# Sixteen rows of a weight matrix loaded early by GpSimd, to shift work between the DMA engines of a decode attention kernel

## The chip, the cores and the metric

The program runs on one core of one Trainium2 chip. The time is the device time of that core for one execution, in microseconds (us), as the median of several runs. The "span" of a profile runs from the first to the last instruction and is some 2 us shorter than the device time.

## The reference

One query token goes through grouped attention over a cache of 65,536 keys, and in parallel through a small dense layer. Cut to what matters:

```python
# x: (1, 1, 512); k_cache, v_cache: (1, 8, 65536, 128); wq: (512, 4096); wo: (4096, 512); all bf16
xn = layernorm(x)
q  = (xn @ wq) as 32 heads of 128          # 4 query heads share one K/V head
p  = softmax(q . k * 128**-0.5)
o  = p . v                                 # 32 x 128
out = x + o.reshape(4096) @ wo + dense_gelu(xn)
```

K and V are 268 MB, all weights together 12 MB. Nothing is used twice, so the kernel has to read 280.5 MB from HBM, the chip's main memory, once.

## The kernel before

SyncE (SP) issues all large loads in one order: K part, K part, V pair, and so on, and wo last. K has two slots and V two slots in one large buffer. The first slots of the same buffer take wo at the end, when K no longer needs them:

```python
    # WP = [(0, 4), (4, 2), (6, 1)]: wo arrives in parts of 16, 8 and 4 rows of 512 values for each partition
    wo_sb = kv[:, 0:GE * HPG * D].rearrange("p (r n) -> p r n", n=D)
    ...
    def dma_wo():
        for i, (g0, n) in enumerate(WP):
            r = n * HPG
            sch.dma(SP, lambda g0=g0, n=n, r=r: sp.dma_start(
                out=wo_sb[:, g0 * HPG:g0 * HPG + r, :],
                in_=A_wo[g0 * HPG * DH:(g0 + n) * HPG * DH, :].rearrange("(p r) n -> p r n", r=r)),
                wsem[i], writes=[f"wo{i}"] + (["slot0"] if i == 0 else []))
        # ... two small parts for the last K/V head follow
```

So the first part of wo is 128 rows of 16 KB each (the packet record of the kernel before has them as 128 packets of 16,384 bytes), one for each of the 128 partitions that the kernel uses in the on-chip buffer that loads are written to, SBUF. GpSimd (POOL) does nothing in the loop but a tiny memset (0.09 us), a "flag", when the second half of a V pair has landed. TensorE reads that half only after the flag:

```python
    def ready_v(res):
        sch.op(POOL, lambda: pool.memset(flag[:, :], 0.0), reads=[res], writes=["v_odd"])
```

The times of the flags are therefore a good clock: one for each of the 16 pairs of K and V.

Of the kernel before, what the change touches and what calls it, by code (L numbers as in the profile page):

```python
# [5 lines left out]
BF = mybir.dt.bfloat16  # L6
# [231 lines left out]
def bass_parallel_sum__gqa_block_cached__dense_activation_gelu__decode_kernel(  # L238
# [13 lines left out]
    D = A_x.shape[-1]  # L252
    DH = 128
    H = A_wq.shape[1] // DH
    G = A_k_cache.shape[1]
    HPG = H // G
# [25 lines left out]
    sch = _Sched(nc)  # L282
# [3 lines left out]
    POOL = sch.add_engine("pool", "pool")  # L286
    SP = sch.add_engine("sp", "sp")
# [7 lines left out]
    pool = nc.gpsimd  # L295
    sp = nc.sync

    def sb(name, shape, dt):
        return nc.alloc_sbuf_tensor(name, shape, dt)
# [25 lines left out]
    kv = sb("kv", [128, NSLOT * TPD * DH], BF)  # L325
# [8 lines left out]
    GE = G - 1  # L334
    WP = []
    g0 = 0
    while g0 < GE:
        n = next(m for m in (4, 2, 1) if g0 + m <= GE)
        WP.append((g0, n))
        g0 += n  # L340
    wo_sb = kv[:, 0:GE * HPG * D].rearrange("p (r n) -> p r n", n=D)
    wl_at = TPD * DH
    wl_sb = kv[:, wl_at:wl_at + HPG * D].rearrange("p (h n) -> p h n", h=HPG)
    kt_ring = sb("kt_ring", [128, NKT * BCOL], BF)
# [20 lines left out]
    oX_bf = sb("oX_bf", [128, GE * HPG], BF)  # L365
# [21 lines left out]
    sem_w2 = sch.dsem("dw2")  # L387
    wsem = [sch.dsem(f"wsem{i}") for i in range(len(WP))]
    lsem = [sch.dsem(f"lsem{i}") for i in range(2)]
    sem_vb = sch.dsem("dvb")  # L390
    sem_out = sch.dsem("dout")

    sch.op(POOL, lambda: pool.memset(sums_all[:, :], 1.0), writes=["sums_all"])
    for t, res in ((ident_bf, "ident_bf"), (ident_f, "ident_f")):
# [4 lines left out]
                out=t[:, :], in_=t[:, :], compare_op=ALU.not_equal, fill=1.0,  # L399
# [49 lines left out]
    def done_chunk(b):  # L449
        free.add(b)  # L450
        issue_chunks()
# [20 lines left out]

    WH = (HPG - 1, 1)

    def dma_wo():
        for i, (g0, n) in enumerate(WP):
            r = n * HPG
            sch.dma(SP, lambda g0=g0, n=n, r=r: sp.dma_start(
                out=wo_sb[:, g0 * HPG:g0 * HPG + r, :],
                in_=A_wo[g0 * HPG * DH:(g0 + n) * HPG * DH, :].rearrange("(p r) n -> p r n", r=r)),  # L480
                wsem[i], writes=[f"wo{i}"] + (["slot0"] if i == 0 else []))
        h0 = 0
        for i, n in enumerate(WH):
            sch.dma(SP, lambda h0=h0, n=n: sp.dma_start(
                out=wl_sb[:, h0:h0 + n, :],
                in_=A_wo[(H - HPG + h0) * DH:(H - HPG + h0 + n) * DH, :].rearrange("(h p) n -> p h n", p=128)),
                lsem[i], writes=[f"wl{i}"] + (["slot1"] if i == 0 else []))
            h0 += n
# [94 lines left out]
    def transposes(b, s):  # L583
        blk = b * BPC + s
        for t in range(TPB):
            fill = (blk * TPB + t) // 8
            tb, at = fill % NPT, t % 8
            sch.op(
                PE,
                lambda tb=tb, at=at, b=b, tt=s * TPB + t: pe.transpose(  # L590
                    pst[tb][:, at * 128:(at + 1) * 128], slot[b][:, tt, :], ident_bf[:, :]),
                reads=[f"slot{b}", "ident_bf"], writes=[f"pst{tb}"], publish=at == 7,
            )
            if at == 7:
                kb, q = blk % NKT, t // 8
                dst = kt_ring[:, kb * BCOL + q * 1024:kb * BCOL + (q + 1) * 1024]
                if fill % 8 in (0, 2, 3, 5, 6):
                    e, fn = DVE, lambda tb=tb, dst=dst: dve.tensor_copy(out=dst, in_=pst[tb][:, :])  # L598
                else:
                    e, fn = ACT, lambda tb=tb, dst=dst: act.activation(out=dst, in_=pst[tb][:, :],  # L600
                                                                      func=ACTF.Copy)
                sch.op(e, fn, reads=[f"pst{tb}"], writes=[f"kt{kb}_{q}"])
# [28 lines left out]
    def load_q(i):  # L631
        sch.op(DVE, lambda: dve.tensor_copy(out=q_cur[:, :], in_=qT_bf[:, at_pair(i, HPG, 0, HPG)]),
               reads=["qT"], writes=["q_cur"])


    def stats_1():
        sch.op(PE, lambda: pe.matmul(pA[0:HPG, PA_ST:PA_ST + 128], lhsT=pmax[:, 0:HPG], rhs=ident_f[:, :],  # L637
                                     start=True, stop=True), reads=["pmax", "ident_f"], writes=["pA"])
        sch.op(DVE, lambda: dve.tensor_reduce(out=gmax4[:, :], in_=pA[0:HPG, PA_ST:PA_ST + 128], axis=AX.X,  # L639
                                              op=ALU.max), reads=["pA"], writes=["gmax"])  # L640
        sch.op(DVE, lambda: dve.tensor_scalar(out=diag4[:, :], in0=ident_f[0:HPG, 0:HPG],  # L641
                                              scalar1=gmax4[0:HPG, 0:1], scalar2=None, op0=ALU.mult),
               reads=["gmax", "ident_f"], writes=["diag"])

    def stats_2(u):
        k = u % 2
        us = slice(k * HPG, (k + 1) * HPG)
        sch.op(PE, lambda: pe.matmul(pA[:, PA_SB:PA_SB + HPG], lhsT=ones_f[0:HPG, 0:128],  # L648
                                     rhs=diag4[0:HPG, 0:HPG], start=True, stop=True),
               reads=["diag", "ones_f"], writes=["pA"])  # L650
        sch.op(DVE, lambda us=us: dve.tensor_scalar(out=negm[:, us], in0=pA[:, PA_SB:PA_SB + HPG],  # L651
                                                    scalar1=-1.0, scalar2=None, op0=ALU.mult),
               reads=["pA"], writes=[f"negm{k}"])
        src = pss[k][:, 0:CW].rearrange("p (t j) -> p t j", j=HPG)
        for j in range(HPG):
            at = k * HPG + j
            sch.op(
                ACT,
                lambda k=k, at=at, j=j, src=src: act.activation(  # L659
                    out=P_v[k][:, :, j], in_=src[:, :, j], func=ACTF.Exp,  # L660
                    bias=negm[:, at:at + 1], scale=1.0, accum_out=sums[:, at:at + 1]),
                reads=[f"negm{k}", f"pss{k}"],
                writes=[f"P{k}_{j}", f"sums{at}"],
            )
        if k:
            i = u // 2
            sch.op(DVE, lambda: dve.tensor_copy(out=negm_all[:, at_pair(i, PW, 0, PW)], in_=negm[:, :]),
                   reads=["negm0", "negm1"], writes=["negm_all"])
# [3 lines left out]
    def keep_sums(i):  # L672
        sch.op(DVE, lambda: dve.tensor_copy(out=sums_all[:, at_pair(i, PW, 0, PW)], in_=sums[:, :]),  # L673
               reads=[f"sums{at}" for at in range(PW)], writes=["sums_all"])
# [21 lines left out]
    def total():  # L696
        sch.op(PE, lambda: pe.matmul(pA[:, PA_SUM:PA_SUM + NC], lhsT=ones_f[:, :], rhs=sums_all[:, :],  # L697
                                     start=True, stop=True), reads=["ones_f", "sums_all"], writes=["pA_sum"])
# [40 lines left out]
    def body(i):  # L739
        last = i == NU // 2 - 1  # L740
        for b in range(2):
            u = 2 * i + b
            transposes(b, 0)
            if b:
                stats_1()
            transposes(b, 1)
            if b:
                stats_2(u - 1)
            else:
                load_q(i)  # L750
            transposes(b, 2)
            scores(b, 0)
            transposes(b, 3)
            done_chunk(f"K{b}")
            for q in range(1, BPC):
                scores(b, q)
        stats_1()
        stats_2(2 * i + 1)
        if last:
            weigh_1()  # L760
        keep_sums(i)
        pv(2 * i)
        total()
        if last:
            weigh_2()
            weigh_3(0, GE, "oT")
            spread()
        pv(2 * i + 1)
# [9 lines left out]
    for i, (_, n) in enumerate(WP):  # L778
        r = n * HPG
        for t, res, pat in ((part_m[i], f"part_m{i}", "p (a r) -> p a r"), (part_r[i], f"part_r{i}", "p (a r) -> p r a")):  # L780
            sch.op(DVE, lambda t=t, pat=pat, r=r: dve.tensor_reduce(
                out=t[:, :], in_=ident_f[:, :].rearrange(pat, r=r), axis=AX.X, op=ALU.max),
                reads=["ident_f"], writes=[res])
    marks, marks2 = [], []
    for i in range(NU // 2):
        marks.append(len(PE.ops))
        marks2.append((len(DVE.ops), len(ACT.ops)))
        assert not (DVE.pending or ACT.pending)
        body(i)
    marks.append(len(PE.ops))  # L790


    for i, (g0, n) in enumerate(WP):
        r = n * HPG
# [9 lines left out]
    def fin_mm(kt, lhsT, rhs, reads, first, last, publish):  # L804
        sch.op(PE, lambda: pe.matmul(pR[32 * kt:32 * kt + 1, 0:128], lhsT=lhsT, rhs=rhs, start=first, stop=last),  # L805
               reads=reads, writes=[f"pss{R}"], publish=publish)
# [3 lines left out]
    for i, (g0, n) in enumerate(WP):  # L810
        for r in range(g0 * HPG, (g0 + n) * HPG):
            for kt in range(KT):
                fin_mm(kt, oX_bf[:, r:r + 1], wo_sb[:, r, kt * 128:(kt + 1) * 128], ["oX", f"wo{i}"], False, False,
                       r == (g0 + n) * HPG - 1 and kt == KT - 1)
    for h in range(HPG):
        for kt in range(KT):
# [61 lines left out]
```

## Time and profile before

| | before |
|---|---|
| device time, median of 3 | 658.36 us (658.20 to 658.52) |
| span | 656.5 us |
| moved by DMA | 280.65 MB, 427 GB/s over the span |
| distance of the flags in the loop | 38.78 us |

Lines of the profile page of the kernel before: the DMA rows (busy tenths of the 16 DMA engines and GB/s in 40 equal slices), the queues (packets, MB, share of 16 engines' span), and the chain of work that ended last.

```profile
DMA  8999999999999999999999999999999999999997
GB/s 369 438 436 426 429 430 433 439 425 461 401 441 439 421 453 413 437 427 445 433 417 449 417 445 421 427 457 411 447 419 447 429 419 441 423 459 408 431 433 295
...
q1 hardware_dynamic: 8616, 280.50, 99.2%
q8 instruction: 8, 0.13, 0.1%
...
DMA 63%; PE 34%; issue 2%; DVE 0%; SPq 0%
...
kv<-in_A_wo_dram SPq DMA_DIRECT2D x1, 2048.0 KB, 23.0
```

The DMA engines are busy from the head to the tail: 9 tenths in 38 of 40 slices. The next fence is the timeline of GpSimd in the kernel before (start, duration, instruction, then the idle time before it and what ended it).

```profile
178.42 0.09 POOL L447 MEMSET flag<- 1x1 f32 x1 [38.69 <-DMA kv<-in_A_v_cache_dram]
217.20 0.11 POOL L447 MEMSET flag<- 1x1 f32 x1 [38.69 <-DMA kv<-in_A_v_cache_dram]
255.97 0.09 POOL L447 MEMSET flag<- 1x1 f32 x1 [38.66 <-DMA kv<-in_A_v_cache_dram]
294.75 0.09 POOL L447 MEMSET flag<- 1x1 f32 x1 [38.69 <-DMA kv<-in_A_v_cache_dram]
333.52 0.09 POOL L447 MEMSET flag<- 1x1 f32 x1 [38.69 <-DMA kv<-in_A_v_cache_dram]
...
605.00 0.09 POOL L447 MEMSET flag<- 1x1 f32 x1 [38.69 <-DMA kv<-in_A_v_cache_dram]
643.86 0.09 POOL L447 MEMSET flag<- 1x1 f32 x1 [38.77 <-DMA kv<-in_A_v_cache_dram]
```

The flags come every 38.78 us, and 16.78 MB in 38.78 us is 433 GB/s: the same as the stage table below shows, with a DMA share of 1.00. The loop runs at the pace of the DMA engines.

The trace holds one more thing that the views above don't print: the record of every DMA packet (start, duration, bytes, queue) and the arrival of the sixteen completion counts of a transfer. I read them as one from each of the page's 16 DMA engines; the record doesn't name the engine. One 32 KB packet takes 1.216 us in the median, one of 16 KB 0.614 us. If 16.78 MB, which is 512 packets of 32 KB, are shared evenly by 16 engines, that is 32 x 1.216 = 38.9 us for a pair; 38.78 us were measured. The counts of one K transfer of the kernel before (landing at 286.7 us), in us before the last of the sixteen:

```
2.00 1.98 1.96 1.94 1.87 1.81 1.76 1.63 | 1.07 | 0.48 0.36 0.30 0.26 0.10 0.10 0
```

By that reading seven engines are late, eight are 1.6 to 2.0 us ahead, one is between. That pattern stands from about 110 us to the end (the first wo transfer, the last to land). The chain above ends with that transfer, at 653.41 us of the span, so its last count sets the end, and this was the target of the change.

### The profile page before, as it was taken

To read this page: it belongs to the slowest core of one execution; us is meant where nothing else is said; L and a number is where in the kernel's file an instruction comes from. 1 tells how busy PE (TensorE), PEld (TensorE's weight loads), DVE (VectorE), ACT (ScalarE), POOL (GpSimd) and SP (SyncE) were. 2 spreads that over 40 slices of the span, in tenths; PEclk is the share of its full clock that TensorE was granted. 3 is DMA by queue.
4 is the path that set the end of the run, shared out by engine and by line. 5 is a ranking of instruction groups with operands and counts; after the bars stand their busy time and mean duration, and the time that the engine had idled before them with its cause. 6 is when DMAs were issued, how large, how long until landed. Compare 5 with 4: busy or idle time off the path is not lost.

```text
span 656.5 us, 27968 instructions
## 1 busy us (share of the span) xinstructions
PE 539.3 (82%) x12682; PEld 512.1 (78%) x12682; DVE 275.7 (42%) x574; ACT 244.9 (37%) x454; POOL 2.9 (0%) x27
## 2 busy tenths in 40 slices
PE   2388699999789797878969787896978879797897
PEld 0187698988689697868969786896968779686896
DVE  3244162635435172442616245171634516254353
ACT  0134153534425152351605335161443516144251
POOL 0000000000000000000000000000000000000000
PEclk9788597878759596885959778596877859687595
DMA  8999999999999999999999999999999999999997
GB/s 369 438 436 426 429 430 433 439 425 461 401 441 439 421 453 413 437 427 445 433 417 449 417 445 421 427 457 411 447 419 447 429 419 441 423 459 408 431 433 295
DMA packets 8774, 280.65 MB, mean 427 GB/s; under 512 B 1082, under 2 KB 1596, under 8 KB 1724
## 3 DMA queue, kind: packets, MB, share of 16 engines
q1 hardware_dynamic: 8616, 280.50, 99.2%
q8 instruction: 8, 0.13, 0.1%
q10 hardware_dynamic: 148, 0.01, 0.0%
q14 instruction: 2, 0.02, 0.0%
HBM read 280.50 MB, written 0.00 MB: 427 GB/s over the span
## 4 chain that ended last, share of the span: by engine, by line
DMA 63%; PE 34%; issue 2%; DVE 0%; SPq 0%
DMA kv<-in_A_k_cache_dram 61%; PE pst L590 27%; PE pss L610 4%; DMA kv<-in_A_wo_dram 3%; PE pO L681 2%; PE pA L637 0%; PE pA L648 0%; DVE pmax L618 0%; PE pA L697 0%; PE pss L805 0%; DVE gmax L639 0%; DVE diag L641 0%; SPq L470 0%; SPq L467 0%; SPq L463 0%
## 5 line engine op out<-in xcount | busy, mean ns | idle before, releaser
L590 PE MATMUL pst<-ident_bf,kv 128*128 128x128 bf16 x4096 | 284.3, 236 | 34.0 <-DMA kv<-in_A_k_cache_dram 33.9
L600 ACT ACTIVATE kt_ring<-pst 128x1024 bf16<-128x1024 bf16 x192 | 195.6, 1027 | 312.1 <-PE pst L590 310.7
L590 PEld LDWEIGHTS pst<-ident_bf,kv 128*128 128x128 bf16 x4096 | 266.0, 107 | 42.4 <-DMA kv<-in_A_k_cache_dram 35.5
L598 DVE COPY kt_ring<-pst 128x1024 bf16<-128x1024 bf16 x320 | 210.7, 687 | 121.1 <-PE pst L590 118.7
L681 PE MATMUL pO<-P_bf,kv 128*128 128x4 bf16 x4096 | 115.1, 166 | 37.1 <-DMA kv<-in_A_v_cache_dram 32.1
L681 PEld LDWEIGHTS pO<-P_bf,kv 128*128 128x128 bf16 x4096 | 113.6, 104 | 38.5 <-DMA kv<-in_A_v_cache_dram 33.1
L610 PE MATMUL pss<-q_cur,kt_ring 128*128 128x4 bf16 x4096 | 111.9, 164 | 4.9 <-issue 4.9
L610 PEld LDWEIGHTS pss<-q_cur,kt_ring 128*128 128x128 bf16 x4096 | 109.3, 96 | 5.1 <-issue 5.1
L659 ACT ACTIVATE P_bf<-pss,negm 128x128 bf16<-128x128 f32 x128 | 50.9, 547 | 67.6 <-DVE negm L651 67.6
L690 DVE COPY o_all<-pO 128x4 f32 (+1 forms) x32 | 5.2, 161 | 120.3 <-PE pO L681 119.5
L618 DVE TENSOR_REDUCE pmax<-pss 128x4 f32<-128x512 f32 x32 | 22.1, 691 | 68.8 <-PE pss L610 68.8
L659 ACT ACTIVATION_READ_ACCUMULATOR P_bf<-pss,negm 128x1 f32 x128 | 35.3, 276 | 0.0
L648 PEld LDWEIGHTS pA<-diag,ones_f 4*128 4x128 f32 x64 | 12.6, 245 | 17.8 <-DVE diag L641 16.2
L637 PE MATMUL pA<-ident_f,pmax 128*4 128x128 f32 x64 | 14.0, 305 | 12.5 <-DVE pmax L618 12.5
L648 PE MATMUL pA<-diag,ones_f 4*128 4x4 f32 x64 | 15.4, 309 | 10.0 <-DVE diag L641 10.0
L637 PEld LDWEIGHTS pA<-ident_f,pmax 128*4 128x4 f32 x64 | 2.9, 84 | 15.7 <-DVE pmax L618 14.0
L639 DVE TENSOR_REDUCE gmax<-pA 4x1 f32<-4x128 f32 x32 | 8.8, 274 | 9.1 <-PE pA L637 9.1
L673 DVE COPY sums_all<-sums 128x8 f32 (+1 forms) x16 | 2.7, 171 | 23.4 <-ACT P_bf L659 23.4
L697 PE MATMUL pA<-sums_all,ones_f 128*128 128x128 f32 x32 | 12.4, 491 | 0.0
L651 DVE TENSOR_SCALAR negm<-pA 128x4 f32<-128x4 f32 x32 | 5.1, 161 | 10.8 <-PE pA L648 10.8
L697 PEld LDWEIGHTS pA<-sums_all,ones_f 128*128 128x128 f32 x32 | 8.1, 312 | 0.0
L641 DVE TENSOR_SCALAR diag<-ident_f,gmax 4x4 f32<-4x4 f32 x32 | 7.0, 218 | 1.1
(78 smaller groups left out, 49.5 us busy)
## 6 DMA issues: line engine op xcount, KB each, us to landing
kv<-in_A_k_cache_dram SPq DMA_DIRECT2D x32, 4096.0 KB, 27.5
kv<-in_A_v_cache_dram SPq DMA_DIRECT2D x4, 4096.0 KB, 23.2
kv<-in_A_wq_dram SPq DMA_DIRECT2D x1, 4096.0 KB, 12.2
kv<-in_B_w_dram SPq DMA_DIRECT2D x2, 1792.0 KB, 18.0
kv<-in_A_wo_dram SPq DMA_DIRECT2D x1, 2048.0 KB, 23.0
kv<-in_A_wo_dram SPq DMA_DIRECT2D x1, 1024.0 KB, 25.1
kv<-in_A_wo_dram SPq DMA_DIRECT2D x1, 512.0 KB, 25.9
kv<-in_A_wo_dram SPq DMA_DIRECT2D x1, 384.0 KB, 16.4
```

Of the source, the lines that this page charges most:

```text
L590: lambda tb=tb, at=at, b=b, tt=s * TPB + t: pe.transpose(pst[tb][:, at * 128:(at + 1) * 128], slot[b][:, tt, :], ident_bf[:, :]),
L598: e, fn = DVE, lambda tb=tb, dst=dst: dve.tensor_copy(out=dst, in_=pst[tb][:, :])
L600: e, fn = ACT, lambda tb=tb, dst=dst: act.activation(out=dst, in_=pst[tb][:, :], func=ACTF.Copy)
L610: lambda k=k, kb=kb, at=at, t=t: pe.matmul(pss[k][:, at:at + HPG], lhsT=kt_ring[:, kb * BCOL + t * 128:kb * BCOL + (t + 1) * 128], rhs=q_c ...
L618: lambda k=k: dve.tensor_reduce(out=pmax[:, :], in_=pss[k][:, 0:CW].rearrange("p (t j) -> p j t", j=HPG), axis=AX.X, op=ALU.max),
L637: sch.op(PE, lambda: pe.matmul(pA[0:HPG, PA_ST:PA_ST + 128], lhsT=pmax[:, 0:HPG], rhs=ident_f[:, :], start=True, stop=True), reads=["pmax" ...
L639: sch.op(DVE, lambda: dve.tensor_reduce(out=gmax4[:, :], in_=pA[0:HPG, PA_ST:PA_ST + 128], axis=AX.X, op=ALU.max), reads=["pA"], writes=[" ...
L641: sch.op(DVE, lambda: dve.tensor_scalar(out=diag4[:, :], in0=ident_f[0:HPG, 0:HPG], scalar1=gmax4[0:HPG, 0:1], scalar2=None, op0=ALU.mult) ...
L648: sch.op(PE, lambda: pe.matmul(pA[:, PA_SB:PA_SB + HPG], lhsT=ones_f[0:HPG, 0:128], rhs=diag4[0:HPG, 0:HPG], start=True, stop=True), reads ...
L659: lambda k=k, at=at, j=j, src=src: act.activation(out=P_v[k][:, :, j], in_=src[:, :, j], func=ACTF.Exp, bias=negm[:, at:at + 1], scale=1.0 ...
L681: lambda k=k, t=t: pe.matmul(pO[:, 0:HPG], lhsT=vslot[:, k * TPD + t, :], rhs=P_v[k][:, t, :], start=t == 0, stop=t == TPD - 1),
L697: sch.op(PE, lambda: pe.matmul(pA[:, PA_SUM:PA_SUM + NC], lhsT=ones_f[:, :], rhs=sums_all[:, :], start=True, stop=True), reads=["ones_f", ...
```

## The change

Its intent is to level the engines. The first part of wo gets a buffer of its own. SyncE loads only 112 of its 128 rows. The other sixteen rows are loaded long before, by GpSimd, in one-row transfers; between any two of them stands a transfer of 34 bytes, so that (by intent) the rows fall on every second DMA engine, two on each, and the short transfers on the rest. The odd lengths (8179 and 17 values are prime) are meant to keep a transfer from being cut up over several engines.

```diff
+    NS = 16
+    ODD = 0
+    spare = sb("spare", [1, 17 * NS], BF)
+    WA = WP[0][1] * HPG
+    LP = WA * D - 13
+    wa = sb("wa", [128, WA * D], BF)
+    wo_sb = kv[:, WA * D:GE * HPG * D].rearrange("p (r n) -> p r n", n=D)
 ...
+    def dma_rest():
+        for n in range(2 * NS):
+            p = 128 - NS + n // 2
+            if n % 2 == ODD:
+                sch.dma(POOL, lambda p=p: pool.dma_start(out=wa[p:p + 1, 0:LP], in_=src_wa()[p:p + 1, 0:LP]), sem_wa,
+                        writes=["wo0r"], total=32 * NS)
+            else:
+                sch.dma(POOL, lambda n=n: pool.dma_start(out=spare[:, n // 2 * 17:n // 2 * 17 + 17], in_=src_wa()[0:1, 0:17]), sem_wa,
+                        writes=["wo0r"], total=32 * NS)
+        sch.dma(SP, lambda: sp.dma_start(out=wa[128 - NS:128, LP:WA * D],
+                                           in_=src_wa()[128 - NS:128, LP:WA * D]), sem_wb, writes=["wo0s"])
 ...
     def dma_wo():
         for i, (g0, n) in enumerate(WP):
+            if i == 0:
+                sch.dma(SP, lambda: sp.dma_start(out=wa[0:128 - NS, :], in_=src_wa()[0:128 - NS, :]), wsem[i],
+                        writes=["wo0"])
+                continue
 ...
+        if i == 4:                         # before the body of the fifth pair
+            dma_rest()
         body(i)
 ... (the last products read wa instead of wo_sb for these rows)
```

More of the change, by code (lines that the diff above doesn't have):

```diff
@@ L340, in bass_parallel_sum__gqa_block_cached__dense_activation_gelu__decode_kernel, with wo_row @@
         g0 += n
-    wo_sb = kv[:, 0:GE * HPG * D].rearrange("p (r n) -> p r n", n=D)
+    NS = 16
[5 more added lines that the diff above has]
+    wo_sb = kv[:, WA * D:GE * HPG * D].rearrange("p (r n) -> p r n", n=D)
+    def wo_row(r, cols):
+        return wa[:, r * D + cols.start:r * D + cols.stop] if r < WA else wo_sb[:, r - WA, cols]
     wl_at = TPD * DH
@@ L389, in bass_parallel_sum__gqa_block_cached__dense_activation_gelu__decode_kernel @@
     lsem = [sch.dsem(f"lsem{i}") for i in range(2)]
+    sem_wa, sem_wb = sch.dsem("dwa"), sch.dsem("dwb")
     sem_vb = sch.dsem("dvb")
@@ L473, in bass_parallel_sum__gqa_block_cached__dense_activation_gelu__decode_kernel, with src_wa @@
     WH = (HPG - 1, 1)
+    def src_wa():
+        return A_wo[0:WA * DH, :].rearrange("(p r) n -> p (r n)", r=WA)
+    def dma_rest():
[9 more added lines that the diff above has]
+                                           in_=src_wa()[128 - NS:128, LP:WA * D]), sem_wb, writes=["wo0s"])
     def dma_wo():
@@ L477, in dma_wo @@
             r = n * HPG
+            if i == 0:
+                sch.dma(SP, lambda: sp.dma_start(out=wa[0:128 - NS, :], in_=src_wa()[0:128 - NS, :]), wsem[i],
+                        writes=["wo0"])
+                continue
             sch.dma(SP, lambda g0=g0, n=n, r=r: sp.dma_start(
-                out=wo_sb[:, g0 * HPG:g0 * HPG + r, :],
+                out=wo_sb[:, g0 * HPG - WA:g0 * HPG - WA + r, :],
                 in_=A_wo[g0 * HPG * DH:(g0 + n) * HPG * DH, :].rearrange("(p r) n -> p r n", r=r)),
-                wsem[i], writes=[f"wo{i}"] + (["slot0"] if i == 0 else []))
+                wsem[i], writes=[f"wo{i}"] + (["slot0"] if i == 1 else []))
         h0 = 0
@@ L812, in bass_parallel_sum__gqa_block_cached__dense_activation_gelu__decode_kernel @@
             for kt in range(KT):
-                fin_mm(kt, oX_bf[:, r:r + 1], wo_sb[:, r, kt * 128:(kt + 1) * 128], ["oX", f"wo{i}"], False, False,
+                fin_mm(kt, oX_bf[:, r:r + 1], wo_row(r, slice(kt * 128, (kt + 1) * 128)), ["oX", f"wo{i}"] + ["wo0r", "wo0s"] * (i == 0), False, False,
                        r == (g0 + n) * HPG - 1 and kt == KT - 1)
```

## The prediction

> **What bounds the kernel now.** The 16 DMA engines. The page gives 280.65 MB in a span of 656.5 us, 427 GB/s, with DMA at 9 tenths in nearly every slice. One 32 KB packet takes 1.214 us on its engine; the loop over K and V repeats every 38.78 us for 16.78 MB (433 GB/s in the stage table). The chain of waits ends on a DMA of wo that lands at 653.41; some 3 us follow (products, cast, store). SP issues the first wo transfer at 625.6, but V is still landing until 643.9: the queue never runs dry, so the wait of 12.7 us for slot 0 costs nothing.
>
> **What is left to win: the spread between engines.** The trace has 16 completion counts per transfer. At 33 us they lie within 0.53 us; from 112 us on within 2.04 us, in a fixed pattern. In the last wo transfer: 0, 0.09, 0.11, 0.23, 0.34, 0.37, 0.46, then 0.86, 0.94, then 1.65 to 1.85 us before the last. The setback comes between 38 and 95 us, where the instruction queue moves seven packets of 16,384 bytes, about 1.05 us each. [...] My reading: seven engines carried such a block and stay 1.2 to 1.7 us behind to the end, and the kernel ends with the slowest. Ideal levelling gains about 0.8 us.
>
> **What the change does.** Before, each engine loads eight 16 KB rows of the first wo transfer. After, 112 rows give seven per engine, and sixteen go by GpSimd, two to each of eight engines. A row is 0.607 us (half of a 32 KB packet), so eight engines lose 0.607 us of work and eight gain it. [...] If the relieved half is the late half, the last count comes 0.25 to 0.6 us earlier (the engines now 0.86 and 0.94 early become the limit if they get rows). If it is the other half, the end is 0.6 us later.
>
> **What it adds.** 32 GpSimd issues after the fifth pair's V has landed (217.2 us). [...] Small packets here cost 9 to 45 ns, so I estimate 0.3 to 1.4 us per engine, all on the bottleneck. GpSimd's next flag is due 38.8 us later; PE has roughly 13 us of slack before the DMA queue runs dry. Only over 1.6 us per issue would cost time. The earlier wo and its own buffer are worth nothing. PE, DVE and ACT are unchanged.
>
> **Prediction.** Gain 0.3 to 0.6, cost 0.2 to 1: 658.1 us, range 657.3 to 659.9. Faster by over 2%: 0.003; within 2%: 0.972; slower: 0.025.
>
> **Right if:** the loop period stays 38.78 us; the span differs by under 1.5 us; the last wo transfer's counts lie closer, 1.0 to 1.4 us instead of 1.85; the GpSimd issues take under 50 us together, and no flag delays V.
>
> **Wrong if:** the issues take over 52 us and the odd PV products stall once (up to 12 us); the rows fall on the late engines (spread 2.5 to 3 us); GpSimd's counts or descriptors cost the engines several us; extra instruction fetches move the late engines.

Gain 0.3 to 0.6 us, cost 0.2 to 1 us, on 658.4 us before, came to 658.1 us. The gain rests on the rows falling on the engines in turn, two on each of eight: an assumption of mine that no trace showed. The cost is my estimate of 32 small writes on each engine, one for each transfer, at 9 to 45 ns (the medians of packets of 4 and of 1024 bytes in the kernel before). One small write on each engine for each transfer fits the kernel before: its queue q1 has 932 packets of 4 bytes, and 58 of its transfers have sixteen counts, 928 in all. The seven packets of 16,384 bytes ("such a block"): that they set seven engines back is my reading.

## The result, and the profile after

The changed kernel takes 679.68 us in the median of four runs (678.52 to 681.83), against 658.37 us before. The ratio is 1.0328, with a 95% interval of 1.030 to 1.0355. It is slower by 21.3 us, and the prediction of 658.1 (657.3 to 659.9) was wrong. The profiled run was the slowest of the four (span 679.9 us); the others had spans from 676.7 to 678.4.

The same lines of the page, changed kernel:

```profile
DMA  8999999999999999999989999999999999999993
GB/s 368 434 458 409 429 432 443 432 422 441 422 441 428 432 421 415 439 416 383 430 364 432 414 450 411 447 407 453 426 409 397 424 432 413 451 424 419 434 294 115
...
q1 hardware_dynamic: 8632, 280.24, 97.4%
q0 software_dynamic: 1024, 0.27, 0.2%
q8 instruction: 8, 0.13, 0.1%
...
DMA 65%; PE 32%; issue 2%; DVE 0%; SPq 0%
...
wa<-in_A_wo_dram SPq DMA_DIRECT2D x1, 1792.0 KB, 41.7
...
wa<-in_A_wo_dram POOLq DMA_DIRECT2D x16, 16.0 KB, 42.0
spare<-in_A_wo_dram POOLq DMA_DIRECT2D x16, 0.0 KB, 44.0
```

Two readings. The last two slices move only 294 and 115 GB/s: most of the 16 engines have nothing left to do there (the DMA share is 0.14 after 666.95 us, in the stage table below). And a row of 16 KB, where a 16 KB packet of the kernel before took 0.614 us, lands 42 us (median) after its issue. The timeline of GpSimd in the changed kernel shows when the loss came:

```profile
178.54 0.09 POOL L458 MEMSET flag<- 1x1 f32 x1 [38.68 <-DMA kv<-in_A_v_cache_dram]
217.36 0.09 POOL L458 MEMSET flag<- 1x1 f32 x1 [38.73 <-DMA kv<-in_A_v_cache_dram]
217.91 0.65 POOL L493 DMA_DIRECT2D wa<-in_A_wo_dram  x1 [0.46 <-issue]
218.55 0.52 POOL L496 DMA_DIRECT2D spare<-in_A_wo_dram  x1
...
233.83 0.52 POOL L496 DMA_DIRECT2D spare<-in_A_wo_dram  x1
260.88 0.09 POOL L458 MEMSET flag<- 1x1 f32 x1 [26.54 <-DMA kv<-in_A_v_cache_dram]
306.34 0.09 POOL L458 MEMSET flag<- 1x1 f32 x1 [45.37 <-DMA kv<-in_A_v_cache_dram]
349.00 0.09 POOL L458 MEMSET flag<- 1x1 f32 x1 [42.57 <-DMA kv<-in_A_v_cache_dram]
387.80 0.09 POOL L458 MEMSET flag<- 1x1 f32 x1 [38.71 <-DMA kv<-in_A_v_cache_dram]
...
622.69 0.09 POOL L458 MEMSET flag<- 1x1 f32 x1 [38.67 <-DMA kv<-in_A_v_cache_dram]
666.95 0.09 POOL L458 MEMSET flag<- 1x1 f32 x1 [44.17 <-DMA kv<-in_A_v_cache_dram]
```

GpSimd needs 0.52 us for an issue, 16.4 us for all 32, and is idle again at 234.35, 26.5 us before the next flag. It delays nothing itself: each flag waits for a DMA of V. But V lands late three times in a row, 43.5, 45.5 and 42.7 us after the one before instead of 38.8. That is 15.3 us (131.64 - 3 x 38.78). The last interval is 44.26 us where it was 38.86, 5.4 us more. The rest, some 2 us, is spread between 388 and 623 us in this slowest of the four runs, and I did not trace it.

The stage table shows that the engines are not short of work in the first stretches: columns are the stretch, its length, busy us of each engine with instruction counts, the granted clock, the DMA share and GB/s. First the kernel before, then the changed one.

```profile
217.20:255.97 38.77, 32.63 (x780) 31.47 (x781) 16.39 (x34) 15.07 (x28) 0.11 (x1) 0.76 1.00 433
...
605.00:643.86 38.86, 35.35 (x861) 34.25 (x862) 17.19 (x35) 15.18 (x29) 0.09 (x1) 0.76 1.00 429
```

```profile
217.36:260.88 43.52, 32.60 (x780) 31.32 (x781) 16.31 (x33) 15.08 (x28) 16.52 (x33) 0.74 1.00 424
260.88:306.34 45.46, 32.36 (x780) 30.98 (x781) 16.31 (x33) 15.08 (x28) 0.09 (x1) 0.73 1.01 427
306.34:349.00 42.66, 32.80 (x780) 31.63 (x781) 16.31 (x33) 15.09 (x28) 0.09 (x1) 0.74 0.97 410
349.00:387.80 38.80, 32.07 (x780) 30.69 (x781) 16.27 (x33) 15.09 (x28) 0.09 (x1) 0.76 0.94 397
...
622.69:666.95 44.26, 37.26 (x908) 35.86 (x908) 19.73 (x45) 15.19 (x29) 0.09 (x2) 0.73 1.00 372
666.95:679.90 12.95, 7.91 (x267) 6.51 (x267) 1.01 (x6) 0.00 (x0) 0.09 (x1) 0.63 0.14 46
```

The compute engines do the same work as before. After 666.95 the mean engine is busy for 14% of the time: about two of sixteen. And between 622.69 and 666.95 the engines are busy all the time (1.00) but move only 372 GB/s, so packets have become slower there.

The completion counts say who was late. K transfers of the changed kernel, in us before the last of the sixteen, from before the GpSimd transfers (first line) to after them:

```
landing at 208 us:   2.09  2.08  2.07  2.00  1.87  1.87  1.84  1.76  0.94  0.42  0.36  0.34  0.32  0.30  0.22  0
landing at 295 us:  10.71 10.69 10.59 10.50 10.44 10.44 10.37  9.33  8.81  8.68  8.67  8.46  7.70  6.31  6.24  0
landing at 340 us:  16.79 16.76 16.65 16.63 16.49 16.42 15.62 15.37 15.13 15.04 15.02 14.82 12.66 12.62 12.27  0
landing at 652 us:   8.97  8.96  8.94  8.71  8.18  8.02  7.99  7.97  7.87  7.81  7.72  7.35  7.20  7.15  6.43  0
```

By these counts one single engine falls behind by some 16 us, while the GpSimd transfers run. (These DMA times have an origin 10.4 us before the span's; in the kernel before it is 11.4 us.) The gap then closes to about 8 us, not because the late engine catches up, but because the program waits for all sixteen counts before it uses a transfer and gives its slot of K or V free again, so the others are made to wait: the DMA share falls to 0.97 and 0.94 between 306 and 388 us. Another record agrees: GpSimd's queue has 1024 packets. 16 are rows of 16,358 bytes, 16 are of 34 bytes, and 992 are of 4 bytes: 31 for each of the 32 transfers. Sixteen of the 31 would be the completion counts (the trace has 512 of them for the 32 transfers), and fifteen one packet for each engine without data: my reading, which fits data on one engine.

### The profile page after: what moved, and what is told of

It reads as the page before. It is cut to its first block, busy times and chain, and to the rows that moved or that the text cites. A ratio compares the mean times of both kernels' runs of the same rounds, so it can differ in the third digit from the quotient of the medians.

```text
span 679.9 us, 28002 instructions
## 1 busy us (share of the span) xinstructions
PE 536.1 (79%) x12682; PEld 508.2 (75%) x12682; DVE 275.4 (41%) x574; ACT 245.0 (36%) x454; POOL 19.3 (3%) x59
## 3 DMA queue, kind: packets, MB, share of 16 engines
q0 software_dynamic: 1024, 0.27, 0.2%
## 4 chain that ended last, share of the span: by engine, by line
DMA 65%; PE 32%; issue 2%; DVE 0%; SPq 0%
DMA kv<-in_A_k_cache_dram 62%; PE pst L620 25%; PE pss L640 4%; DMA kv<-in_A_wo_dram 3%; PE pO L711 2%; PE pA L667 0%; PE pA L678 0%; DVE pmax L648 0%; PE pA L727 0%; DVE gmax L669 0%; PE pss L837 0%; DVE diag L671 0%; SPq L481 0%; SPq L478 0%; SPq L474 0%
## 5 line engine op out<-in xcount | busy, mean ns | idle before, releaser
L620 PE MATMUL pst<-ident_bf,kv 128*128 128x128 bf16 x4096 | 280.6, 234 | 41.7 <-DMA kv<-in_A_k_cache_dram 41.6
L620 PEld LDWEIGHTS pst<-ident_bf,kv 128*128 128x128 bf16 x4096 | 262.4, 106 | 49.8 <-DMA kv<-in_A_k_cache_dram 43.1
L678 PEld LDWEIGHTS pA<-diag,ones_f 4*128 4x128 f32 x64 | 12.6, 244 | 18.5 <-DVE diag L671 16.8
L458 POOL MEMSET flag<- 1x1 f32 x16 | 1.4, 88 | 646.4 <-DMA kv<-in_A_v_cache_dram 646.4
L493 POOL DMA_DIRECT2D wa<-in_A_wo_dram x16 | 8.4, 526 | 0.5 <-issue 0.5
```

Of the source, the lines that this page charges most:

```text
L493: sch.dma(POOL, lambda p=p: pool.dma_start(out=wa[p:p + 1, 0:LP], in_=src_wa()[p:p + 1, 0:LP]), sem_wa, writes=["wo0r"], total=32 * NS)
L620: lambda tb=tb, at=at, b=b, tt=s * TPB + t: pe.transpose(pst[tb][:, at * 128:(at + 1) * 128], slot[b][:, tt, :], ident_bf[:, :]),
L678: sch.op(PE, lambda: pe.matmul(pA[:, PA_SB:PA_SB + HPG], lhsT=ones_f[0:HPG, 0:128], rhs=diag4[0:HPG, 0:HPG], start=True, stop=True), reads ...
```

## The experiments

The theories at the start. A: all GpSimd transfers put their data on one and the same DMA engine, which costs 15 us, and the 112-row transfer itself is slow, which costs 6. B: the transfers are spread, but each costs every engine a fixed time. C: the buffer, with its earlier issue, spoils the end. Each experiment starts from the changed kernel. "dup" experiments let SyncE load all 128 rows again at the end, so that the early rows are pure extra work and the end is as before; the result stays right. All results were correct.

| run | what differs | this, us | before, us | ratio (95%) |
|---|---|---|---|---|
| own_buffer | buffer alone | 658.48 | 658.45 | 1.0001 (0.9984 to 1.0018) |
| split_112_16 | 112 + 16 rows, all by SyncE | 665.28 | 658.45 | 1.0100 (1.0083 to 1.0116) |
| no_short | no 34 byte transfers | 678.82 | 658.45 | 1.0321 (1.0300 to 1.0343) |
| dup_rows | 32 transfers, then 128 rows | 674.22 | 658.45 | 1.0240 (1.0223 to 1.0257) |
| dup_by_sp | 16 single rows by SyncE | 677.40 | 658.31 | 1.0292 (1.0275 to 1.0309) |
| short_only | 32 short transfers, no rows | 658.62 | 658.31 | 1.0004 (0.9988 to 1.0021) |
| dup_pairs | 8 transfers of 2 rows | 667.30 | 658.31 | 1.0142 (1.0125 to 1.0159) |
| dup_once | 1 transfer of 16 rows | 661.97 | 658.31 | 1.0054 (1.0037 to 1.0071) |
| foreign_8 | 8 rows to partitions 112 to 119 | 665.25 | 658.35 | 1.0103 (1.0088 to 1.0119) |
| own_8 | 8 rows to 0 to 3, 32 to 35 | 661.67 | 658.35 | 1.0050 (1.0034 to 1.0065) |
| split_64_64 | 64 + 64 rows by SyncE | 664.85 | 658.35 | 1.0097 (1.0081 to 1.0112) |
| half_8 | 1 transfer of 8 rows, to partitions 0, 4, ... 28 | 658.74 | 658.35 | 1.0006 (0.9992 to 1.0019) |
| own_dst_far_src | written as own_8, read as foreign_8 | 661.61 | 658.49 | 1.0048 (1.0033 to 1.0064) |
| far_dst_own_src | written as foreign_8, read as own_8 | 665.24 | 658.49 | 1.0102 (1.0086 to 1.0117) |
| columns | an eighth early, as columns | 658.46 | 658.49 | 0.9999 (0.9986 to 1.0013) |

### own_buffer: the buffer alone

```diff
     def dma_rest():
-        ... (all of it)
+        pass
-                sch.dma(SP, lambda: sp.dma_start(out=wa[0:128 - NS, :], in_=src_wa()[0:128 - NS, :]), wsem[i],
-                        writes=["wo0"])
+                sch.dma(SP, lambda: sp.dma_start(out=wa[:, :], in_=src_wa()), wsem[i], writes=["wo0"])
```

Expected:

> The own buffer alone: all 128 rows of the first wo part in one SyncE transfer, nothing from GpSimd. Theory A (all the GpSimd transfers put their data on one and the same DMA engine, which costs some 15 us, and the transfer of 112 rows runs at half speed, which costs some 6 us): 658.0 to 658.8 us, flags 38.8 us apart to the end, 16 KB packets near 614 ns. Theory B (the 32 GpSimd transfers are spread as intended, but each costs every engine fixed time): the same. Theory C (the buffer, with the wo transfer issued 12 us earlier, causes the 5.5 us lost between the last two flags): 663 to 665 us.

Measured: 658.48 us, the last two flags 38.84 us apart, 16 KB packets 614 ns. The buffer and the issue 12 us earlier cost nothing and win nothing. Theory C is out.

### split_112_16: the 112-row transfer without GpSimd

```diff
     def dma_rest():
-        ... (all of it)
+        pass
                 sch.dma(SP, lambda: sp.dma_start(out=wa[0:128 - NS, :], in_=src_wa()[0:128 - NS, :]), wsem[i],
                         writes=["wo0"])
+                sch.dma(SP, lambda: sp.dma_start(out=wa[128 - NS:128, :], in_=src_wa()[128 - NS:128, :]), sem_wa,
+                        writes=["wo0r"])
```

Expected:

> 112 rows and 16 rows as two late SyncE transfers, nothing from GpSimd. Theory A: 16 KB packets of the 112 rows take about 1160 ns as in the changed kernel, so the last part grows by 7 times 0.55 us, some 3 to 5 us: 661 to 663.5 us, with the flags still 38.8 us apart. Theory B: 658 to 659 us. Theory C: 663 to 665 us, as with the buffer alone.

Measured: 665.28 us, 6.8 us slower, more than expected. The 16 KB packets take 1157 ns in the median instead of 614; in the changed kernel, 1160. So the same bytes took nearly twice as long when they went to 112 partitions. I had missed that this also slows what is still running: the last flag came at 646.03 instead of 643.86, so the end of V was delayed by 2.2 us.

### no_short and dup_rows: which part makes one engine late

The first cuts the `else` branch with the short transfers. The second keeps all 32 transfers and restores the 128-row load:

```diff
-        sch.dma(SP, ... out=wa[128 - NS:128, LP:WA * D] ... sem_wb, writes=["wo0s"])
 ...
-                sch.dma(SP, lambda: sp.dma_start(out=wa[0:128 - NS, :], in_=src_wa()[0:128 - NS, :]), wsem[i],
-                        writes=["wo0"])
+                sch.dma(SP, lambda: sp.dma_start(out=wa[:, :], in_=src_wa()), wsem[i], writes=["wo0", "wo0r"])
```

Expected of no_short:

> The changed kernel without the 34 byte transfers: sixteen GpSimd transfers of one row. If the turn moves on by one engine at each transfer, every engine gets one row, no engine falls behind, and the flags stay 38.8 us apart: below 665 us. Theory A (all rows on one engine whatever is sent between): that engine is again over 9 us behind the others, 675 to 679 us. Theory B: half of the fixed costs, near 669 us, with no single engine behind.

Expected of dup_rows:

> The 32 GpSimd transfers of the changed kernel as they are, but SyncE then loads all 128 rows again in one transfer (the same data, so the result is right). Theory A: the loss of 15 to 16 us between 217 and 349 us stays, the last two flags are 38.8 us apart, one engine is 8 to 10 us behind: 673 to 676 us. Theory B: the loss is there without one engine behind. Theory C: the last two flags are 44 us apart, 679 us.

Measured: without the short transfers 678.82 us, one engine 16.8 us behind at the peak. Nothing moved on from one transfer to the next, with or without something between. dup_rows takes 674.22 us, as theory A expected. Its GpSimd timeline has the early loss (260.73, 306.08, 348.74) but not the late one:

```profile
620.72 0.09 POOL L458 MEMSET flag<- 1x1 f32 x1 [38.69 <-DMA kv<-in_A_v_cache_dram]
659.66 0.09 POOL L458 MEMSET flag<- 1x1 f32 x1 [38.85 <-DMA kv<-in_A_v_cache_dram]
```

The last interval is 38.94 us instead of 44.26. So the late loss belongs to the 112-row load, and the early loss, 15.8 us (674.22 - 658.45), to the rows on one engine.

### short_only: the price of a GpSimd transfer without data

```diff
-            if n % 2 == ODD: ... (the rows)
+            sch.dma(POOL, lambda n=n: pool.dma_start(out=spare[:, n * 17:n * 17 + 17], in_=src_wa()[0:1, 0:17]), sem_wa,
+                    writes=["wo0r"], total=32 * NS)
```

Expected:

> 128 rows by SyncE in one transfer, and early 32 GpSimd transfers of 34 bytes each, no rows. Theory A (bytes of the rows on one engine): 658.3 to 659.5 us, no engine more than 3 us behind. Theory B (a fixed cost of each GpSimd transfer, which I had estimated before the change at 0.3 to 1.4 us for all): over 665 us would be needed to explain the loss.

Measured: 658.62 us, ratio 1.0004. The 992 extra packets of 4 bytes (median 9 ns each in the changed kernel) are next to free. Theory B is out; the difference of 0.3 us is the lower end of my estimate and lies within the noise.

### dup_pairs and dup_once: where a transfer of several partitions goes

```diff
+        for n in range(NS // 2):          # dup_pairs
+            p = 128 - NS + 2 * n
+            sch.dma(POOL, lambda p=p: pool.dma_start(out=wa[p:p + 2, 0:LP], in_=src_wa()[p:p + 2, 0:LP]), sem_wa, ...)
```
```diff
+        sch.dma(POOL, lambda: pool.dma_start(out=wa[128 - NS:128, :], in_=src_wa()[128 - NS:128, :]), sem_wa,   # dup_once
+                writes=["wo0r"])
```

Expected of dup_pairs:

> As dup_rows, but the sixteen rows go in eight GpSimd transfers of two rows. Theory D1 (partition number within the transfer decides: partition 0 to the first engine, partition 1 to the second, always starting at the same one): two engines get eight rows each and are about 8 us late at the peak and 7 us at the end, 16 times the half: 665 to 667.5 us. Theory D2 (all of a small GpSimd transfer on one engine): 674 us. Theory D3 (a turn that moves on by the number of engines used): one row for each engine, 658.5 to 660 us.

Expected of dup_once:

> As dup_rows, but the sixteen rows go in one GpSimd transfer of 16 partitions. Theories D1 and D3: one row on each engine, 0.6 to 1.0 us for all: 658.9 to 659.8 us, counts of every transfer within 2.5 us. Theory D2: 674 us.

Measured: dup_pairs takes 667.30 us. Its counts at 294 us have two late engines: 0 and 1.58 us before the last, then nothing until 5.29. So two rows went to two engines, and eight transfers in a row to the same two. The 4 byte packets agree: 30 for each transfer of two rows, 16 for that of sixteen in dup_once, where one row has 31, so each row more is one packet less. dup_once has no late engine (counts within 2.6 us): with the 16 small packets this reads as one row on each of sixteen engines. But it costs 3.7 us where I expected 0.6 to 1.0, a miss: the sixteen rows took 0.85 to 2.33 us each. That fixes the number of engines, as far as counts can; why a lone row costs more than its bytes is not yet.

### dup_by_sp: the same rows through SyncE's own queue

```diff
+        for n in range(NS):
+            p = 128 - NS + n
+            sch.dma(SP, lambda p=p: sp.dma_start(out=wa[p:p + 1, 0:LP], in_=src_wa()[p:p + 1, 0:LP]), sem_wa,
+                    writes=["wo0r"], total=16 * NS)
```

Expected:

> As dup_rows, but the sixteen one-row transfers are issued early by SyncE instead of GpSimd, and there are no short transfers. One partition means one DMA engine here too. Theory A1 (a row costs its engine its bytes, 0.607 us, plus 0.38 us that the change from one queue's packets to the other's costs): on SyncE's own queue only the bytes remain, 16 times 0.607 = 9.7 us, so 668.2 us (667.3 to 669.2), one engine 9 to 10 us behind. Theory A2 (a lone row costs 0.98 us whatever the queue): 674 us. If SyncE's transfers were spread: below 660 us.

(The 0.98 us are an estimate: the 15.8 us of dup_rows over its sixteen rows; less 0.607 this leaves 0.38.)

Measured: 677.40 us, outside both expectations. One engine is 19.0 us late at the peak, so SyncE's one-row transfers share one engine too, and the rows follow each other at 1.234 us each (median 1234 ns), twice the 0.614 us of a 16 KB packet. With one queue alone the rows were no cheaper, so two queues taking turns is not the cause. What the slow cases may have in common is which partitions they write: 112 to 127, or 112 instead of 128.

### foreign_8, own_8 and split_64_64: the partitions written

The two theories. P: what a row costs beyond its bytes depends on the partitions that it is written to. Q: it is a cost of the change from one queue's packets to the other's. Two assumptions of mine: that rows to partitions 0 to 3 and 32 to 35 cost their bytes alone, and that packets take twice the 0.61 us in a transfer of 64 neighbouring partitions.

```diff
+        for p in (0, 1, 2, 3, 32, 33, 34, 35):      # own_8; foreign_8: (112, ..., 119)
+            sch.dma(POOL, lambda p=p: pool.dma_start(out=wa[p:p + 1, 0:LP], in_=src_wa()[p:p + 1, 0:LP]), sem_wa,
+                    writes=["wo0r"], total=8 * NS)
```
```diff
+                sch.dma(SP, lambda: sp.dma_start(out=wa[0:64, :], in_=src_wa()[0:64, :]), wsem[i],         # split_64_64
+                        writes=["wo0"])
+                sch.dma(SP, lambda: sp.dma_start(out=wa[64:128, :], in_=src_wa()[64:128, :]), sem_wa,
+                        writes=["wo0r"])
```

Expected of foreign_8:

> As dup_rows, but only eight one-row GpSimd transfers, to partitions 112 to 119, and no short ones. Theory P (a row costs its engine the bytes[...]) and theory Q (the change from one queue's packets to the other's costs 0.38 us a row) both: half of the loss of sixteen, 8 times 0.98 = 7.9 us, 666.3 us (665.3 to 667.3).

Expected of own_8:

> The same eight transfers, but to partitions 0 to 3 and 32 to 35[...]. Theory P: [...]only the bytes remain: 8 times 0.61 = 4.9 us, 663.3 us (662.6 to 664.0), row packets near 0.61 us. Theory Q: as foreign_8, 666.3 us, row packets near 0.77 us.

Expected of split_64_64:

> 128 rows of the first wo part as two late SyncE transfers of 64 partitions, nothing from GpSimd. [...]Theory P: 16 KB packets take near 1.21 us instead of 0.61, 8 times 0.6 = 4.8 us, 662.5 to 665.5 us. If only uneven shares like seven rows per engine are slow: 658.5 us and 614 ns.

Measured: the eight row packets take 676 to 800 ns in foreign_8 and 611 to 615 in own_8. 32 KB packets are also stretched in foreign_8 while the rows run: the six that follow a row at once take 1.53 to 1.57 us, and six others 1.37 to 1.84 us. None in own_8 takes over 1.23 us there. The times are 665.25 and 661.67 us. Both lie below what I expected, for one reason that the counts show: the engine that gets the rows is one of the early ones. In own_8 it ends 3.1 us behind the seven late ones, and 8 x 0.61 = 4.9 us of rows less its lead of about 1.75 us is 3.1. Taken with that lead, a row cost its engine 0.61 us when written to partitions 0 to 3 and 32 to 35, and (6.9 + 1.75) / 8 = 1.08 us when written to 112 to 119. split_64_64 takes 664.85 us, 6.5 more than the kernel before, with 16 KB packets of 1174 ns against 614, near the 1.21 us assumed. Its first fifty packets, by the order of issue those of partitions 0 to 63, take 1178 ns too, so it is not the high partitions alone that are slow. Theory P fits all three runs in so far as the partitions written change what a packet costs; by what mechanism they do is not shown, as the trace names no engine, and a lone row from another engine to a low partition was not tried.

Nor is the 112-row load explained. In the changed kernel 104 of the 112 packets took 0.99 us or more (median 1160 against 614 ns). That the transfer is slow is shown by split_112_16; why nearly all of its packets are is open, and so is why the sixteen rows of dup_once took 0.85 to 2.33 us.

### half_8: which engines are the late ones

```diff
+        sch.dma(POOL, lambda: pool.dma_start(out=wa[0:32:4, :], in_=src_wa()[0:32:4, :]), sem_wa,
+                writes=["wo0r"])
```

Expected:

> 128 rows by SyncE in one transfer, and one early GpSimd transfer of eight partitions (0, 4, ... 28): by what dup_pairs showed it gives one row to each of the first eight engines[...]. Those eight lose 0.61 us. If the engines that are late anyway (seven, by 1.2 to 1.7 us) are among them, the end is 0.6 us later: 658.9 to 659.3 us, and in the counts of one transfer the gap between the two groups grows by 0.6 us. If the late ones are the other eight: 658.3 to 658.6 us, the gap shrinks by 0.6 us, and rows moved to the first eight engines would be a small gain. If mixed: 658.9 us with four groups.

Measured: 658.74 us, ratio 1.0006; the eight rows took 613 to 616 ns, the bytes alone, and 24 packets of 4 bytes, as sixteen counts and one for each of eight engines without a row, fit one row on each of eight engines. The late counts before and after the transfer:

```
landing at 208 us:  0.84 | 0.29 0.26 0.18 0.11 0.07 0.06 0
landing at 286 us:  0.83 0.76 0.72 0.65 0.60 0.54 0.19 0
```

If the 0.61 us is added to the engines at 0.84, 0.26 and 0.07, the second line comes out to 0.01 us. Of all 12,870 choices of eight of the sixteen counts, the 294 that come within 0.15 us all put the delay on two of the seven late ones. So by this matching two of the seven late engines are among the eight that got a row and five are not. That is my inference from times, not a record of engine numbers. If those eight are neighbours (assumed, not shown), it would also mean that the late engines are not every second one, as that would put three or four of the seven among the eight; then even two rows on each of every second engine would not have levelled them. No transfer tried here was seen to reach every second engine, so this was not tested.

### own_dst_far_src, far_dst_own_src and columns: the last doubt, and a clean way

own_8 and foreign_8 differ in the partitions written and also in the rows read. Two runs cross them. A third takes an eighth of the part out early as columns of all partitions:

```diff
+        for p, q in zip((0, 1, 2, 3, 32, 33, 34, 35), range(112, 120)):     # and the other way round
+            sch.dma(POOL, lambda p=p, q=q: pool.dma_start(out=wa[p:p + 1, 0:LP], in_=src_wa()[q:q + 1, 0:LP]), sem_wa, ...)
```
```diff
+        sch.dma(POOL, lambda: pool.dma_start(out=wa[:, 7168:8192], in_=src_wa()[:, 7168:8192]), sem_wa,     # columns
+                writes=["wo0r"])
 ...
+                sch.dma(SP, lambda: sp.dma_start(out=wa[:, 0:7168], in_=src_wa()[:, 0:7168]), wsem[i],
```

Expected of own_dst_far_src:

> Eight one-row GpSimd transfers to partitions 0 to 3 and 32 to 35, read from the rows that belong to partitions 112 to 119 (SyncE writes the right rows over them later, so the result is right). If the partitions written decide: as own_8, row packets near 0.61 us and 661.7 us (661.2 to 662.2). If the rows read decide: as foreign_8, 665.2 us, packets near 0.77 us.

Expected of far_dst_own_src:

> The cross: partitions 112 to 119 written, rows 0 to 3 and 32 to 35 read. If the partitions written decide: as foreign_8, 665.2 us (664.7 to 665.8). If the rows read decide: 661.7 us.

Expected of columns:

> The same share of bytes (an eighth of the first wo part) taken out early by one GpSimd transfer, but as 2 KB of each of the 128 partitions; SyncE loads the other 14 KB of each. All shares equal[...]: 658.2 to 658.7 us, as before; no 14 KB packet over 0.56 us. It cannot level the engines, so it should not beat the kernel before. If an early GpSimd transfer costs by itself: over 659.5 us.

Measured: 661.61 us with row packets of 611 ns, and 665.24 us with 770 ns (medians). The partitions written decided, the rows read didn't. columns takes 658.46 us with no 14 KB packet over 0.548 us: early loading by GpSimd cost nothing when the share was the same for each of the 128 partitions (658.46 against 658.49 us). As the expectation said, it can't beat the kernel before, and it doesn't. No experiment pointed to a version that would.

## Why the prediction was wrong

- **The bound: right.** The DMA engines bound both kernels (DMA share 1.00 in the loop before). In the changed kernel it is one of them (16.8 us behind at the peak).
- **The wait for slot 0 and the own buffer are worth nothing: right.** own_buffer takes 658.48 against 658.45 us.
- **The assumed placement, one-row transfers of GpSimd on one engine after the other: wrong, and this is the step that failed first.** The changed kernel has one late engine (16.8 us), no_short gives the same lateness, dup_pairs gives two late engines. So I read that in these runs the engine depended on the place of the partition within its transfer, and that each transfer started anew at the same engine. (On which engine the 34 bytes of a short transfer went can't be seen.) The packets of 4 bytes agree with one engine: 31 for each one-row transfer, 30 for two rows, 24 for eight, 16 for sixteen. Cost: 15.8 us (dup_rows), where the prediction had no more than 0.6 us for badly placed rows.
- **"A row is 0.607 us": right for some partitions, wrong here.** A row measured 0.61 us to partitions 0 to 3 and 32 to 35 (own_8) and, by estimate from the counts, about 1.08 us to 112 to 119 (foreign_8); the row packets of the changed kernel, to 112 to 127, took 658 to 818 ns, 772 in the median. The sixteen rows then cost 16 x 1.1 less the lead of 1.75 us, which is the 15.8 us.
- **"112 rows give seven per engine": the second step that failed, as I priced them at full speed.** (Seven per engine fits the 112 packets, but the trace doesn't name the engines.) They ran at 1160 ns for 16 KB instead of 614, for a reason that stays open. That is the other 5.5 us (679.68 - 674.22), and 6.8 us alone (split_112_16). In the changed kernel it hurts through the late engine: it was still loading V while the others wrote wo. In the packet records I followed it by matching ends and starts in time: five of its 32 KB packets then took 2.1 to 2.6 us instead of 1.21, 5.4 us more in all, which is what the last flag came late (44.26 against 38.86 us).
- **GpSimd's issues: right.** 0.52 us each, under the 50 us named, and no flag was held up by them.
- **Small writes, 0.3 to 1.4 us: the low end.** short_only differs by 0.3 us, within its interval.
- **The range was too narrow because both outcomes that I weighed kept the rows spread.** Among the ways to fail I named rows on the late engines, at 0.6 us. I did not ask what happens if the unproven placement doesn't hold at all: sixteen rows on one engine, 16 x 0.607 less 0.607 = 9.1 us, or some 7.4 us if it was one of the engines that are ahead, could have been worked out from the same numbers.

Open: the run-to-run spread of the changed kernel (678.5 to 681.8 us, the kernel before 0.3), why single rows cost 1.08 us by GpSimd and 1.23 us by SyncE, why eight rows on each of two engines cost 9.0 us (dup_pairs) and eight on one 6.9 us (foreign_8), why 112 rows are slow (1160 ns for 16 KB), why two loads of 64 are (1174 ns), by what the partitions written change the cost of a row, and which engines are late and why: that the seven packets of 16,384 bytes between 38 and 95 us are the cause was argued from the times (the spread of the counts is 0.53 us before and 2.04 us after them, and stays), not tested.

## What to carry to other kernels

Here all DMA engines were full (share 1.00 in the loop), and a load counted by the engine that got most of it: sixteen rows on one engine cost 15.8 us, and the others were made to wait for it, as the program uses a slot again only when all sixteen counts are in. So before you send single rows or odd numbers of partitions, find out from a trace how they are spread and what a packet takes: 16 KB took 0.61 us in a load of 128 partitions and 1.16 us in one of 112. Look at the sixteen completion counts of a transfer, not at the mean DMA share, which still read 0.97 to 1.01 while one engine fell 16 us behind. To take a share out of a load, take columns of all 128 partitions, which cost nothing here (658.46 against 658.49 us, where eight single rows cost 3.1 to 6.9 us), and price a placement that no trace has shown as if it failed.
